# A fourth buffer for the scan units, a third for v, gathers first in a slot

## The chip, the core and the metric

One NeuronCore of a Trainium2 chip runs the whole program. The metric is device time in microseconds (us). Before the change the median of three runs is 211.96 us, with 209.6 and 213.6 as the extremes.

## The reference

A linear-attention recurrence over four sequences (B = 4), eight heads, 768 steps and head size 48, followed by a soft mixture of experts on its output:

```python
for t in range(S):
    cur = einsum('bhd,bhe->bhde', u * k[t], v[t])
    y[t] = einsum('bhd,bhde->bhe', r[t], state + cur)
    state = w[t][..., None] * state + einsum('bhd,bhe->bhde', k[t], v[t])
x = y.transpose(0, 2, 1, 3).reshape(B * S, H * D)        # 3072 x 384
logits = x @ phi                                         # 3072 x 32, 8 experts of 4 slots
d = softmax over tokens;  slot_input = d.T @ x
for e in range(8):
    slot_out[e] = relu(slot_input[e] @ w1[e]) @ w2[e]    # 384 -> 1024 -> 384
out = softmax over slots(logits) @ slot_out
```

Everything is float32.

## The kernel before

The recurrence is cut into chunks of 128 steps, six to a sequence. Decays are turned into running products by scans on VectorE; keys are divided by them and queries multiplied, so that each chunk becomes masked matmuls plus a small state that is carried from chunk to chunk.

**Groups and units.** A sequence has eight heads, worked as four *groups* of two heads (NG = 4); n = 0 to 15 counts the groups of all four sequences. One head takes 48 of 64 partitions, so two heads leave 2 x 16 partitions free. The host packs the fourth group's two heads into these free rows of the first three. So a sequence needs only three *units* of scanning (NU = 3, twelve units in all; `unit(n)` gives a group's unit), and the fourth group's keys and queries are collected afterwards into two tiles of their own, `k3` and `r3`, by `a_gather`: four small DMAs a unit (two from `ld` into `k3`, two from `rt` into `r3`), each from 16 partitions to 16 others.

**Buffers.** `lds` holds a unit's decays and keys (128 x 1550), `rts` its queries (128 x 774); there are three of each, and unit i sits in buffer i % 3. `a_load` fills an `ld`, `a_load_r` an `rt`. `vt` holds a group's values, in a pool of two. VectorE overwrites `ld` and `rt` in place (`a_back` and `a_fwd`, each once for either half h of a unit): the gathers read what `a_fwd(i, 1)` leaves.

**The slots.** The order of all instructions is written out by hand. One pass of the loop over `it` (0 to 16) is called a slot. It scans for the unit of group `it`, does the matmuls of group n = it - 1, and carries the finished output of group m = it - 2 on. In the TensorE order of a slot stand:

- `b_kn` (L292): transposes of the keys, in two halves, which ScalarE copies out (L293, L296);
- `b_scores` (L307): the scores, in two halves of twelve matmuls into two PSUM banks each, that ScalarE copies (L311) and GpSimd masks (L312);
- `d_a` (L246), then `b_u` (L323), whose result VectorE scans into the state (L329) and ScalarE copies (L332);
- `l_turn` (L378): transposes of the finished output x;
- `c_av` (L344), `l_part` (L395), `c_inter` (L359) and two filler matmuls (L782).

`ps_t` is a rotation of four PSUM banks that transposes, scores, `d_a`, `l_turn` and `l_part` share. In the slot of a sequence's fourth group (n = 3, 7, 11, 15) there are no transposes of keys, and the scores read `k3` and `r3`.

**The DMA queue.** All DMAs are issued by SyncE (SP) in program order; a DMA that has to wait holds those behind it. At the head of a slot stand `a_load_v(it)`, `a_load_r` of unit(m) + 3, up to two thirds-of-a-tile of the expert weights (`more_weights`, 512 KB each, PER_IT of them), and then the gathers of unit(n); in the middle of the slot follows `a_load` of unit(n) + 3, into the buffer that was just gathered from. A weight tile is 128 x 3072 (1536 KB). There are sixteen, w1 of eight experts and then w2 of eight; nine arrive in the loop (pool `w_a`, N_WA = 9), two when the decays, keys and queries are finished with and their space is free (`w_b`, N_WB = 2), two when the rest of the recurrence's space is free (`w_c`), three into the first tiles of `w_a` when the first layer has used these.

After the loop come the rest of the logits, the experts' two layers (L530 and L566) and the mixing of their output (L595).

Of the kernel before, what the change touches and what calls it, by code (L numbers as in the profile page):

```python
# [9 lines left out]
F32 = mybir.dt.float32  # L10
# [3 lines left out]
AF = mybir.ActivationFunctionType  # L14
ALU = mybir.AluOpType
# [4 lines left out]
P = 128  # L20
# [7 lines left out]
N_WARM_2 = 5  # L28
N_DENSE = 2
N_FILL = (4, 3)  # L30
N_WA = 9
N_WB = 2
N_WC = 2
N_PIECE = 3
PER_IT = (0, 0, 2, 2, 2, 2, 2, 2, 2, 2, 2, 2, 2, 2, 2, 1)
COLS = ((0, 208), (208, 384))

NB = 4
# [14 lines left out]
def rwkv_soft_moe(ctx: ExitStack, tc: tile.TileContext, wkr, v, ublk, phi, w1, w2, out_a, out_b):  # L53
    nc = tc.nc
    NSC, _, LOAD = wkr.shape
    NIT = v.shape[0]
# [8 lines left out]
    NG = H // 2  # L65
# [4 lines left out]
    SCAN = C * E1  # L70
    R_OFF = K_OFF + SCAN
# [7 lines left out]
    attn = ExitStack()  # L79
    early = ExitStack()  # L80
    decay = early.enter_context(tc.tile_pool(name="decay", bufs=1, side="right"))
    fixed = attn.enter_context(tc.tile_pool(name="fixed", bufs=1))
    once = attn.enter_context(tc.tile_pool(name="once", bufs=1))
    vpool = attn.enter_context(tc.tile_pool(name="vpool", bufs=2))
    work = attn.enter_context(tc.tile_pool(name="work", bufs=4))
    xpool = attn.enter_context(tc.tile_pool(name="xpool", bufs=2))
    ps_y = banks.enter_context(tc.tile_pool(name="ps_y", bufs=1, space=PSUM))
# [2 lines left out]
    ps_c = banks.enter_context(tc.tile_pool(name="ps_c", bufs=1, space=PSUM))  # L90


    lds = [decay.tile([P, R_OFF], F32, name=f"ld{n}") for n in range(3)]
    rts = [decay.tile([P, SCAN], F32, name=f"rt{n}") for n in range(3)]

    def a_load(i, lo=0, hi=R_OFF):
        nc.sync.dma_start(out=lds[i % 3][:, lo:hi], in_=wkr[i, :, lo:hi])

    def a_load_r(i):
        nc.sync.dma_start(out=rts[i % 3], in_=wkr[i, :, R_OFF:LOAD])  # L100
# [9 lines left out]
    b_one = const.tile([P, 1], F32, name="b_one")  # L110
# [56 lines left out]
    prod = cst[:, 4:]  # L167
    up = ps_u.tile([P, D, C], F32, name="up")

    def by_chunk(t):  # L170
        return t.rearrange("p (c e) -> p c e", e=E1)

    def keys(i):
        return by_chunk(lds[i % 3][:, K_OFF:R_OFF])[:, :, 1:E1]

    def queries(i):
        return by_chunk(rts[i % 3])[:, :, 0:P]

    nc.vector.memset(cst[:, 0:1], 1.0)
    nc.vector.memset(cst[:, 1:2], INV_MAX)  # L180
# [11 lines left out]
    def a_load_v(i):  # L192
        vt = vpool.tile([P, 2, C, D], F32, name="vt")
        nc.sync.dma_start(out=vt, in_=v[i])
        sts[i]["vv"] = vt

    def a_back(i, h):

        t, lo = lds[i % 3], HALF * E1 * h
        nc.vector.tensor_tensor_scan(  # L200
            out=prod[:, ::-1], data0=t[:, lo + 1:lo + 1 + HALF * E1][:, ::-1], data1=one,
            initial=1.0, op0=ALU.mult, op1=ALU.min)

        nc.vector.reciprocal(out=by_chunk(t[:, lo:lo + HALF * E1])[:, :, 0], in_=by_chunk(prod)[:, :, 0])

    def a_fwd(i, h):


        lo = HALF * E1 * h
        k_, r_ = lds[i % 3][:, K_OFF + lo:K_OFF + lo + HALF * E1], rts[i % 3][:, lo:lo + HALF * E1]  # L210
        nc.vector.tensor_tensor(out=k_, in0=k_, in1=prod, op=ALU.mult)  # L211
        nc.vector.tensor_tensor_scan(  # L212
            out=prod, data0=lds[i % 3][:, lo:lo + HALF * E1], data1=big, initial=1.0, op0=ALU.mult, op1=ALU.min)
        nc.vector.tensor_tensor(out=r_, in0=r_, in1=prod, op=ALU.mult)  # L214

    def spread(pat, k_):
        pend = by_chunk(k_)[:, 1:C, 0:1].rearrange("p c o -> p o c")
        nc.scalar.copy(out=pat[:, :, 1:C], in_=pend.broadcast_to([P, D, C - 1]))

    def a_pat(i):  # L220
        spread(pats[i % 2], lds[i % 3][:, K_OFF:R_OFF])

    def a_gather(i):

        lo = PART * (i % NU)
        for dst, src in ((k3, lds[i % 3][:, K_OFF:R_OFF]), (r3, rts[i % 3])):
            for h in range(2):
                nc.sync.dma_start(out=dst[64 * h + lo:64 * h + lo + PART], in_=src[64 * h + D:64 * h + 64])

    def a_end(i):  # L230
        junk6 = small.tile([P, C], F32, name="junk6", bufs=1)
        nc.scalar.activation(out=junk6, in_=by_chunk(rts[i % 3])[:, :, P], func=AF.Abs, bias=b_one,
                             scale=1.0, accum_out=chk[:, i:i + 1])

    def d_rk(i):
# [570 lines left out]
    for it in range(NIT + 1):  # L806
        n, m = it - 1, it - 2
        ph = it % NG
        A, i = it < NIT and ph < NU, unit(it)
        B_ = n >= 0  # L810
        mb, mg = divmod(m, NG)
        X = m >= 0 and mg >= 1
        Y = mg == 0 and mb >= 1
        Z = mg == 1 and mb >= 1
        U_ = B_ and n % NG < NU

        nxt = unit(it + 1) if ph == NU and it + 1 < NIT else None
        if 1 <= it < NIT:
            a_load_v(it)
        if m >= 0 and m % NG < NU and unit(m) + 3 < NSC:  # L820
            a_load_r(unit(m) + 3)
        if it < NIT:
            more_weights(it)
        if U_:
            a_gather(unit(n))
        if it == NIT:
            early.close()
            late = weights.enter_context(tc.tile_pool(name="late", bufs=1, side="right", reuse_waits="tile"))
            w_b = weights.enter_context(tc.tile_pool(name="w_b", bufs=N_WB, side="right", reuse_waits="tile"))
            load_weight(w_b, wts, N_WB)  # L830
            cT = late.tile([P, NT // NB, P], F32, name="cT")
            siT = late.tile([P, E * KT, NS], F32, name="siT")
            nc.gpsimd.memset(siT, 0.0)
        if it == 0:
            masks()
            d_rk(0)
            a_back(0, 0)
            a_fwd(0, 0)
            a_back(0, 1)
            d_a(0)  # L840
            d_a_turn(0)
            keep_warm(N_WARM_2, ps_t, "tp")
            d_rk(1)
        if ph == NU:
            d_a_last(it // NG)
        if B_:
            d_av(n)
            b_kn(n, 0)
            b_scores(n, 0)
            b_kn(n, 1)  # L850
        if m >= 0:
            c_evac(m)
        if A and ph == 0:
# [12 lines left out]
        if U_ and unit(n) + 3 < NSC:
            a_load(unit(n) + 3)
        if A and it:
            d_a(i)
        if B_:  # L870
            b_u(n)
        if Y:
            s_exp(mb - 1, qs[mb - 1])
        if B_:
            if not U_:
                spread(pat3, k3)
            b_state(n)
        if X:
            xT = l_turn(xb[mb], mg - 1, once, ps_t)
            if mg == 1:  # L880
                lts[mb] = small.tile([TG, 2, P], F32, name="lt", bufs=1)
        if Z:
            s_norm(mb - 1, qs[mb - 1])
        if A and ph == 0:
            a_back(i + 1, 0)
            a_fwd(i + 1, 0)
        elif A and ph == 1:
            a_back(i + 1, 0)
            d_rk(i + 1)
        elif A:  # L890
            a_fwd(i, 1)
            if it + 2 < NIT:
                d_rk(i + 1)
        elif nxt is not None:
            a_back(nxt, 1)
            d_rk(nxt + 1)
        if it == 1:
            keep_warm(N_WARM_2, ps_t, "tp")
        if B_:
            c_y(n)  # L900
            c_av(n, 0)
            c_av(n, 1)
        if A and it:
            d_a_turn(i)
        if X:
            l_part(mg - 1, xT, lts[mb], ps_t)
        if A:
            a_pat(i)
            a_end(i)
        if X and mg == NG - 1:  # L910
            qs[mb] = s_max(mb, lts[mb], cst[0:TG, 2:3])
        if Y:
            s_dturn(qs[mb - 1], ps_t)
            s_rows(qs[mb - 1], ps_t)
            s_rows_exp(qs[mb - 1])
        if Z and mb < B - 1:
            s_slots(xb[mb - 1], mb - 1, qs[mb - 1], ps_t)
        if B_:
            c_inter(n, 0)
            c_inter(n, 1)  # L920
        if 1 <= it < NIT:
            keep_dense(N_DENSE)
        if Z and mb < B - 1:
            s_sum(mb - 1, qs[mb - 1])
# [184 lines left out]
```

## Time and profile before

| what | value |
|---|---|
| median of 3 runs | 211.96 us (209.6 to 213.6) |
| the profiled execution | 210.83 us, span of its records 209.1 us |
| busy share of the span | PE 87%, PEld 60%, DVE 58%, ACT 44%, POOL 37% |
| share of 16 DMA engines, HBM read | 69.9%, 44.28 MB |
| mean granted TensorE clock | 0.924 |

The profile names engines PE (TensorE matmuls), PEld (its weight loads), DVE (VectorE), ACT (ScalarE), POOL (GpSimd) and SP (SyncE, which only issues DMAs; SPq is its instruction queue). A row of the timeline or of the groups reads: line and engine, operation, output <- inputs, shape, count. The view of waits reads: who waited, for whom, us in total, how often, the longest. The chain of waits follows the work back from the last instruction; its rows read start, length, what. The view by windows gives busy time of each engine in a stretch, with the granted clock (PEclk, 1.00 is full), the DMA engines' busy share and GB/s as its last three columns.

### The profile page before, as it was taken

What the parts mean: (1) busy time and instruction counts of PE and PEld (TensorE: products, weight loads), DVE (VectorE), ACT (ScalarE), POOL (GpSimd) and SP (SyncE); (2) the same over time, 40 slices, a digit from 0 to 9 for tenths busy, and PEclk for the clock granted to TensorE, in tenths of its full rate; (3) what the DMA queues carried; (4) which work ended last, traced back from release to release, by engine and by line L of the source; (5) the groups of instructions that cost most, each with busy time, mean ns of one, the idle gap of its engine ahead of it and who ended that gap; (6) DMA issues with size and microseconds to landing.
All of it is one profiled execution on the core that took longest, in us unless ns stands there. A gap on an engine that the chain in (4) does not pass through costs nothing.

```text
span 209.1 us, 7275 instructions
## 1 busy us (share of the span) xinstructions
PE 181.7 (87%) x3019; PEld 126.0 (60%) x3019; DVE 122.1 (58%) x237; ACT 92.0 (44%) x266; POOL 77.1 (37%) x133
## 2 busy tenths in 40 slices
PE   7599799699999859999982899999969999999830
PEld 2156678477778737777861687788755423565520
DVE  4399859648789861979976088794132531104440
ACT  2043636355777505777750355678524001103330
POOL 3356356532656453274735315464600300000000
PEclk9979759979999996999999579999996999999995
DMA  6975659679595959949587678466888607954873
GB/s 209 358 280 164 187 187 301 231 282 342 163 330 198 324 202 330 325 146 327 188 284 243 225 276 284 96 225 181 304 326 308 263 13 255 419 235 162 330 311 121
DMA packets 14105, 51.93 MB, mean 248 GB/s; under 512 B 2288, under 2 KB 2416, under 8 KB 13552
## 3 DMA queue, kind: packets, MB, share of 16 engines
q1 hardware_dynamic: 14064, 51.38, 69.9%
q8 instruction: 26, 0.43, 0.8%
q14 instruction: 15, 0.12, 0.2%
HBM read 44.28 MB, written 4.72 MB: 234 GB/s over the span
## 4 chain that ended last, share of the span: by engine, by line
PE 67%; DMA 13%; DVE 10%; ACT 2%; issue 2%; SPq 1%; POOL 1%; ACTq 0%; DVEq 0%; POOLq 0%
PE ap L307 14%; DMA r<-rt 10%; PE y L344 8%; PE hp L530 5%; PE so L566 5%; PE tp L378 5%; PE y L359 5%; PE up L323 4%; PE tp L292 3%; PE aps L246 3%; DMA rt<-in_wkr_dram 3%; PE lp L395 3%; PE op L595 2%; DVE cst L200 2%; DVE cst L212 2%
## 5 line engine op out<-in xcount | busy, mean ns | idle before, releaser
L312 POOL TENSOR_SCALAR_AFFINE_SELECT at<-at 128x384 f32<-128x384 f32 x64 | 31.7, 521 | 36.7 <-ACT at L311 36.7
L311 ACT COPY at<-ap 128x384 f32<-128x384 f32 x64 | 27.4, 484 | 25.9 <-PE ap L307 24.9
L307 PE MATMUL ap<-rt,ld 48*128 48x128 f32 x288 | 27.6, 303 | 0.0
L344 PE MATMUL y<-vt,at 128*64 128x48 f32 x768 | 26.6, 228 | 0.0
L344 PEld LDWEIGHTS y<-vt,at 128*64 128x64 f32 x768 | 24.8, 143 | 2.6 <-issue 2.2
L238 POOL TENSOR_TENSOR rk<-rt,ld 128x384 f32<-128x384 f32 x24 | 20.2, 861 | 16.0 <-DMA rt<-in_wkr_dram 14.6
L307 PEld LDWEIGHTS ap<-rt,ld 48*128 48x128 f32 x288 | 22.5, 196 | 4.5 <-issue 4.0
L329 DVE TENSOR_TENSOR_SCAN Sb<-up,pat 112x288 f32<-112x288 f32 x16 | 12.1, 755 | 22.5 <-PE up L323 15.5
L278 POOL TENSOR_TENSOR av<-vt,a 128x576 f32<-128x576 f32 x16 | 18.4, 1151 | 17.0 <-ACT a L257 17.0
L200 DVE TENSOR_TENSOR_SCAN cst<-ld,cst 128x387 f32<-128x387 f32 x24 | 22.9, 954 | 1.6 <-DMA ld<-in_wkr_dram 1.4
L212 DVE TENSOR_TENSOR_SCAN cst<-ld,cst 128x387 f32<-128x387 f32 x24 | 23.2, 968 | 0.8
L332 ACT COPY Sn<-Sb 112x240 f32<-112x240 f32 x16 | 10.1, 632 | 17.4 <-DVE Sb L329 17.4
L307 PE MATMUL ap<-r,k 48*128 48x128 f32 x96 | 9.3, 348 | 9.0 <-DMA r<-rt 9.0
L369 DVE TENSOR_TENSOR x<-y,av 128x576 f32<-128x576 f32 x16 | 12.1, 755 | 6.9 <-PE y L359 5.5
L211 DVE TENSOR_TENSOR ld<-ld,cst 128x387 f32<-128x387 f32 x24 | 13.0, 543 | 3.4 <-POOL rk L238 3.4
L307 PEld LDWEIGHTS ap<-r,k 48*128 48x128 f32 x96 | 8.4, 251 | 9.9 <-issue 9.7
L214 DVE TENSOR_TENSOR rt<-rt,cst 128x387 f32<-128x387 f32 x24 | 13.4, 558 | 0.8
L323 PEld LDWEIGHTS up<-vt,kn 128*48 128x48 f32 x320 | 9.6, 137 | 6.5 <-issue 1.8
L378 PE MATMUL tp<-ident,x 128*128 128x128 f32 x72 | 12.1, 311 | 1.0 <-DVE x L369 1.0
L293 ACT COPY kn<-tp 128x336 f32<-128x336 f32 (+1 forms) x24 | 9.6, 399 | 7.1 <-PE tp L292 7.1
L566 PE MATMUL so<-wt,hT 128*32 128x208 f32 (+1 forms) x256 | 12.5, 329 | 0.0
L380 ACT COPY xT<-tp 128x384 f32<-128x384 f32 x24 | 10.3, 478 | 3.1 <-PE tp L378 3.0
(132 smaller groups left out, 260.2 us busy)
## 6 DMA issues: line engine op xcount, KB each, us to landing
wt<-in_w_dram SPq DMA_DIRECT2D x27, 512.0 KB, 6.8
ld<-in_wkr_dram SPq DMA_DIRECT2D x11, 775.0 KB, 4.3
wt<-in_w_dram SPq DMA_DIRECT2D x4, 1536.0 KB, 7.7
rt<-in_wkr_dram SPq DMA_DIRECT2D x12, 387.0 KB, 6.0
vt<-in_v_dram SPq DMA_DIRECT2D x16, 288.0 KB, 4.5
wt<-in_w_dram SPq DMA_DIRECT2D x3, 832.0 KB, 6.8
out_dram<-wt SPq DMA_DIRECT2D x3, 832.0 KB, 3.8
wt<-in_w_dram SPq DMA_DIRECT2D x3, 704.0 KB, 10.4
```

The source lines that it names most:

```text
L200: nc.vector.tensor_tensor_scan(out=prod[:, ::-1], data0=t[:, lo + 1:lo + 1 + HALF * E1][:, ::-1], data1=one, initial=1.0, op0=ALU.mult, op ...
L212: nc.vector.tensor_tensor_scan(out=prod, data0=lds[i % 3][:, lo:lo + HALF * E1], data1=big, initial=1.0, op0=ALU.mult, op1=ALU.min)
L214: nc.vector.tensor_tensor(out=r_, in0=r_, in1=prod, op=ALU.mult)
L238: nc.gpsimd.tensor_tensor(out=rks[i % 2].rearrange("p (c e) -> p c e", e=P)[:, part], in0=queries(i)[:, part], in1=keys(i)[:, part], op=AL ...
L278: nc.gpsimd.tensor_tensor(out=av, in0=st["vv"], in1=a.broadcast_to([P, 2, C, D]), op=ALU.mult)
L307: nc.tensor.matmul(out=aps[h][:, cc, :], lhsT=kt_[rows, c * E1 + 1:(c + 1) * E1], rhs=rt_[rows, c * E1:c * E1 + P], start=True, stop=True)
L311: nc.scalar.copy(out=at, in_=aps[h])
L312: nc.gpsimd.affine_select(out=at, in_=at, pattern=[[0, 3], [1, P]], compare_op=ALU.is_gt, fill=0.0, base=0, channel_multiplier=-1)
L323: nc.tensor.matmul(out=up[rows, :, n + 1], lhsT=st["kn"][:, n, rows], rhs=st["vv"][:, h, n, :], start=first[h], stop=(n == C - 2))
L344: nc.tensor.matmul(out=st["y"][cols, h, c * D:(c + 1) * D], lhsT=st["AT", h, hf][:, cc, cols], rhs=st["vv"][:, h, c, :], start=(c == 0), s ...
L378: nc.tensor.transpose(out=tp[:, j, :], in_=x[:, 3 * hf + j, kt * P:(kt + 1) * P], identity=ident)
L566: nc.tensor.matmul(out=so[32 * g:32 * g + NS, :], lhsT=hT[ft // 2][:, ft % 2, e, :], rhs=wts[E + e][:, base + ft * wd:base + (ft + 1) * wd ...
```

## The change

`lds` and `rts` get a fourth buffer each (NL = 4), and the pool of `vt` a third. A unit's `ld` and `rt` are now both issued at the head of slot m + 2 for unit(m) + 4, and v for group it + 1 instead of `it`; before the loop v of group 1 and the `ld` and `rt` of unit 3 are loaded as well. The gathers become the first DMAs of a slot, ahead of v, `ld`, `rt` and weights. The space is taken from the loop's weights: N_WA falls from 9 to 8 and N_WB rises from 2 to 3, so that one w2 tile is loaded after the loop instead of in it (PER_IT has three pieces fewer). In `b_kn` and `b_scores` both halves of the key transposes come ahead of the first half of the scores, except in the first group.

```diff
-N_WA = 9
-N_WB = 2
+N_WA = 8
+N_WB = 3
-PER_IT = (0, 0, 2, 2, 2, 2, 2, 2, 2, 2, 2, 2, 2, 2, 2, 1)
+PER_IT = (0, 0, 2, 2, 2, 1, 2, 2, 2, 1, 2, 2, 2, 1, 2, 1)
+NL = 4
-    vpool = attn.enter_context(tc.tile_pool(name="vpool", bufs=2))
+    vpool = attn.enter_context(tc.tile_pool(name="vpool", bufs=3))
-    lds = [decay.tile([P, R_OFF], F32, name=f"ld{n}") for n in range(3)]
-    rts = [decay.tile([P, SCAN], F32, name=f"rt{n}") for n in range(3)]
+    lds = [decay.tile([P, R_OFF], F32, name=f"ld{n}") for n in range(NL)]
+    rts = [decay.tile([P, SCAN], F32, name=f"rt{n}") for n in range(NL)]
...
     a_load_r(2)
     a_load(2)
+    a_load_v(1)
+    a_load(3)
+    a_load_r(3)
     nc.sync.dma_start(out=phi_sb, in_=phi)
...
-        if 1 <= it < NIT:
-            a_load_v(it)
-        if m >= 0 and m % NG < NU and unit(m) + 3 < NSC:
-            a_load_r(unit(m) + 3)
+        if U_:
+            a_gather(unit(n))
+        if 1 <= it < NIT - 1:
+            a_load_v(it + 1)
+        if m >= 0 and m % NG < NU and unit(m) + NL < NSC:
+            a_load(unit(m) + NL)
+            a_load_r(unit(m) + NL)
         if it < NIT:
             more_weights(it)
-        if U_:
-            a_gather(unit(n))
...
             b_kn(n, 0)
+            if n:
+                b_kn(n, 1)
             b_scores(n, 0)
-            b_kn(n, 1)
+            if not n:
+                b_kn(n, 1)
...
             b_scores(n, 1)
-        if U_ and unit(n) + 3 < NSC:
-            a_load(unit(n) + 3)
```

How the order of instructions moves is seen at three places. The first is SP's queue at the head of the slot of n = 6, whose gathers (unit 5, the third of its sequence) are the last that the fourth group n = 7 needs. Numbers at `ld`, `rt` tell the buffers apart; 97 to 99 are the three `ld` of before. Before:

```order
L97 DMA ld_98<-in_wkr_dram 128x1550
L194 DMA vt<-in_v_dram 128x576
L100 DMA rt_101<-in_wkr_dram 128x774
L153 DMA wt<-in_w_dram 128x1024 x2
L228 DMA k_132<-ld_99 16x774 x2
L228 DMA r_133<-rt_102 16x774 x2
```

And the same slot of the changed kernel, where unit 5 sits in `ld_98` and `rt_102`:

```order
L155 DMA wt<-in_w_dram 128x1024 x2
L230 DMA k_134<-ld_98 16x774 x2
L230 DMA r_135<-rt_102 16x774 x2
L196 DMA vt<-in_v_dram 128x576
L99 DMA ld_97<-in_wkr_dram 128x1550
L102 DMA rt_101<-in_wkr_dram 128x774
L155 DMA wt<-in_w_dram 128x1024 x2
```

The four gathers now stand ahead of the slot's v, `ld`, `rt` and two weight pieces, and directly behind the weight pieces of the slot before. The second place is TensorE's order at the head of the slot of n = 8, before:

```order
L292 MATMUL tp<-ident,ld_97 128x128 x3
L307 MATMUL ap<-rt_100,ld_97 128x128 x6
L292 MATMUL tp<-ident,ld_97 128x128 x2
L307 MATMUL ap<-rt_100,ld_97 128x128 x6
L246 MATMUL aps<-rk_129,u_sb 32x256 x3
L323 MATMUL up<-vt,kn 48x48 x10
```

The same slot of the changed kernel (a float32 matmul of these rows is two instructions in the trace):

```order
L294 MATMUL tp<-ident,ld_99 128x128 x5
L309 MATMUL ap<-rt_103,ld_99 128x128 x12
L248 MATMUL aps<-rk_131,u_sb 32x256 x3
L325 MATMUL up<-vt,kn 48x48 x10
L380 MATMUL tp<-ident,x 128x128 x6
```

The five transposes are now one block ahead of one block of twelve scores. The third place is SP's queue around the end of the loop, before:

```order
L153 DMA wt<-in_w_dram 128x1024
L228 DMA k_132<-ld_99 16x774 x2
L228 DMA r_133<-rt_102 16x774 x2
L145 DMA wt<-in_w_dram 128x3072 x4
L145 DMA wt<-in_w_dram 128x1664 x3
L145 DMA wt<-in_w_dram 128x1408 x3
```

And in the changed kernel:

```order
L230 DMA k_134<-ld_100 16x774 x2
L230 DMA r_135<-rt_104 16x774 x2
L155 DMA wt<-in_w_dram 128x1024
L147 DMA wt<-in_w_dram 128x3072 x5
L147 DMA wt<-in_w_dram 128x1664 x3
L147 DMA wt<-in_w_dram 128x1408 x3
```

One more whole weight tile stands between the last gathers and the six part-tiles that end the weights.

More of the change, by code (lines that the diff above doesn't have):

```diff
@@ L90, in rwkv_soft_moe @@
     ps_c = banks.enter_context(tc.tile_pool(name="ps_c", bufs=1, space=PSUM))
-    lds = [decay.tile([P, R_OFF], F32, name=f"ld{n}") for n in range(3)]
-    rts = [decay.tile([P, SCAN], F32, name=f"rt{n}") for n in range(3)]
+    lds = [decay.tile([P, R_OFF], F32, name=f"ld{n}") for n in range(NL)]
+    rts = [decay.tile([P, SCAN], F32, name=f"rt{n}") for n in range(NL)]
     def a_load(i, lo=0, hi=R_OFF):
-        nc.sync.dma_start(out=lds[i % 3][:, lo:hi], in_=wkr[i, :, lo:hi])
+        nc.sync.dma_start(out=lds[i % NL][:, lo:hi], in_=wkr[i, :, lo:hi])
     def a_load_r(i):
-        nc.sync.dma_start(out=rts[i % 3], in_=wkr[i, :, R_OFF:LOAD])
+        nc.sync.dma_start(out=rts[i % NL], in_=wkr[i, :, R_OFF:LOAD])
     a_load(0, 0, K_OFF)
@@ L173, in keys @@
     def keys(i):
-        return by_chunk(lds[i % 3][:, K_OFF:R_OFF])[:, :, 1:E1]
+        return by_chunk(lds[i % NL][:, K_OFF:R_OFF])[:, :, 1:E1]
     def queries(i):
-        return by_chunk(rts[i % 3])[:, :, 0:P]
+        return by_chunk(rts[i % NL])[:, :, 0:P]
     nc.vector.memset(cst[:, 0:1], 1.0)
@@ L197, in a_back @@
     def a_back(i, h):
-        t, lo = lds[i % 3], HALF * E1 * h
+        t, lo = lds[i % NL], HALF * E1 * h
         nc.vector.tensor_tensor_scan(
@@ L209, in a_fwd @@
         lo = HALF * E1 * h
-        k_, r_ = lds[i % 3][:, K_OFF + lo:K_OFF + lo + HALF * E1], rts[i % 3][:, lo:lo + HALF * E1]
+        k_, r_ = lds[i % NL][:, K_OFF + lo:K_OFF + lo + HALF * E1], rts[i % NL][:, lo:lo + HALF * E1]
         nc.vector.tensor_tensor(out=k_, in0=k_, in1=prod, op=ALU.mult)
         nc.vector.tensor_tensor_scan(
-            out=prod, data0=lds[i % 3][:, lo:lo + HALF * E1], data1=big, initial=1.0, op0=ALU.mult, op1=ALU.min)
+            out=prod, data0=lds[i % NL][:, lo:lo + HALF * E1], data1=big, initial=1.0, op0=ALU.mult, op1=ALU.min)
         nc.vector.tensor_tensor(out=r_, in0=r_, in1=prod, op=ALU.mult)
@@ L220, in a_pat @@
     def a_pat(i):
-        spread(pats[i % 2], lds[i % 3][:, K_OFF:R_OFF])
+        spread(pats[i % 2], lds[i % NL][:, K_OFF:R_OFF])
     def a_gather(i):
         lo = PART * (i % NU)
-        for dst, src in ((k3, lds[i % 3][:, K_OFF:R_OFF]), (r3, rts[i % 3])):
+        for dst, src in ((k3, lds[i % NL][:, K_OFF:R_OFF]), (r3, rts[i % NL])):
             for h in range(2):
@@ L231, in a_end @@
         junk6 = small.tile([P, C], F32, name="junk6", bufs=1)
-        nc.scalar.activation(out=junk6, in_=by_chunk(rts[i % 3])[:, :, P], func=AF.Abs, bias=b_one,
+        nc.scalar.activation(out=junk6, in_=by_chunk(rts[i % NL])[:, :, P], func=AF.Abs, bias=b_one,
                              scale=1.0, accum_out=chk[:, i:i + 1])
@@ L271, in rows_of @@
             return k3, r3
-        return lds[unit(i) % 3][:, K_OFF:R_OFF], rts[unit(i) % 3]
+        return lds[unit(i) % NL][:, K_OFF:R_OFF], rts[unit(i) % NL]
     def d_av(i):
```

## The prediction

> **What bounds the kernel now.** I read the page first, for the busy shares and the chain of work that ended last, then that chain in order of time.
>
> ```profile
> PE 181.7 (87%) x3019; PEld 126.0 (60%) x3019; DVE 122.1 (58%) x237; ACT 92.0 (44%) x266; POOL 77.1 (37%) x133
> PE 67%; DMA 13%; DVE 10%; ACT 2%; issue 2%; SPq 1%; POOL 1%; ACTq 0%; DVEq 0%; POOLq 0%
> 34.83 7.16 DMA r<-rt
> ...
> 71.06 6.72 DMA r<-rt
> ...
> 108.20 7.52 DMA r<-rt
> 115.97 3.02 PE ap L307 x24
> ```
>
> TensorE is the bound, and the only DMA of weight in its chain is the gather of `r3`, three times, 6.7 to 7.5 us each: in front of the fourth groups n = 3, 7 and 11. What TensorE really lost is less, since it had other work for most of that time. The view of waits tells it:
>
> ```profile
> PE ap L307 <- DMA r<-rt: 9.0, 3, 4.7
> ```
>
> So 9.0 us of idle TensorE in three waits, 4.7 the longest. Then I looked at the loop by windows: the slots right behind the three waits, then stretches without one (columns: PE, PEld, DVE, ACT, POOL busy, then clock, DMA share, GB/s).
>
> ```profile
> 42.12:50.74 8.62, 8.62 (x156) 6.84 (x157) 4.95 (x9) 4.75 (x13) 3.09 (x5) 0.80 0.87 313
> 77.92:86.70 8.78, 8.78 (x156) 6.86 (x157) 4.21 (x8) 4.97 (x13) 3.14 (x5) 0.81 0.86 305
> 115.97:126.00 10.03, 10.03 (x156) 7.93 (x157) 4.39 (x8) 4.97 (x13) 3.14 (x5) 0.67 0.77 271
> 86.70:101.85 15.15, 15.15 (x312) 12.02 (x311) 13.42 (x24) 10.41 (x32) 8.31 (x13) 1.00 0.80 270
> 126.00:148.28 22.28, 22.27 (x461) 17.74 (x459) 15.60 (x29) 15.59 (x47) 12.32 (x21) 1.00 0.66 193
> ```
>
> Each wait is paid twice: behind it the granted clock averages 0.80, 0.81 and 0.67 over a slot, and elsewhere in the loop it is 1.00 with TensorE busy all the time (15.15 of 15.15, 22.27 of 22.28).
>
> **Why the gather is late.** SP's rows of the slot of n = 6, and the VectorE row that makes the data ready:
>
> ```profile
> 65.15 0.56 DVE L214 TENSOR_TENSOR rt<-rt,cst 128x387 f32<-128x387 f32 x1
> ...
> 67.34 0.33 SPq L97 DMA_DIRECT2D ld<-in_wkr_dram  x1
> 67.80 0.36 SPq L194 DMA_DIRECT2D vt<-in_v_dram  x1
> 68.33 0.33 SPq L100 DMA_DIRECT2D rt<-in_wkr_dram  x1
> 68.71 1.10 SPq L153 DMA_DIRECT2D wt<-in_w_dram  x2
> 69.85 1.16 SPq L228 DMA_DIRECT2D k<-ld  x2
> 71.06 1.30 SPq L228 DMA_DIRECT2D r<-rt  x2
> SPq L97 <- DMA k<-ld: 37.6, 11, 5.9
> DMA to landing us min/median/max: 2.1/5.6/7.5
> ```
>
> Unit 5 is finished at 65.15 + 0.56 = 65.71, but the gather of `r3` is issued at 71.06. SP first sits on the `ld` load, which waits until the gathers have left its buffer (37.6 us over eleven loads), then issues 775 + 288 + 387 + 2 x 512 = 2474 KB in front of the gather, and these have to move first.
>
> **The change part by part.**
>
> *Gathers first, loads a unit ahead.* `r3`'s gathers can go out two k issues (1.16 us) after 65.71, at about 66.9, instead of 71.06. What is ahead of them is the load of the slot before, issued some 8 us earlier. With even the longest landing, 7.5 us, they are there at 74.4; TensorE's own work before them ends at 75.71 (77.92 less the 2.21 it waited). So the wait of n = 7 goes, with 1.3 us to spare in the worst case and 6.7 in the best (2.1 us). Waits on the old buffer go too: the next `ld` now needs a buffer emptied one slot earlier. The same holds at n = 3 and n = 11, which have the same queue. Gain: 9.0 us, all of that wait. What is then late next: nothing on SP, since v, `ld` and `rt` behind the gathers are needed one slot later than before.
>
> *The clock behind the waits.* At full clock the three slots would take 8.62 x 0.80, 8.78 x 0.81 and 10.03 x 0.67, that is 6.9, 7.1 and 6.7 us; the rest, 1.7 + 1.7 + 3.3 = 6.7 us, is the low clock. That the wait causes it is seen at n = 15, a fourth group without a wait:
>
> ```profile
> 148.61 0.92 PE ap L307 x12
> 42.12 1.13 PE L307 MATMUL ap<-r,k 48*128 48x128 f32 x14 [2.06 <-DMA r<-rt]
> 77.92 0.34 PE L307 MATMUL ap<-r,k 48*128 48x128 f32 x1 [2.21 <-DMA r<-rt]
> ```
>
> Its twelve scores take 0.92 us, where the 24 behind the third wait took 3.02 (chain above). I take all 6.7 us; the bounds are 0 and 6.7. [...]
>
> *The order of transposes and scores* (eleven groups: the twelve with transposes less n = 0). The chain at n = 8, and ScalarE's copy there:
>
> ```profile
> 87.03 0.87 PE ap L307 x12
> 87.89 0.37 PE tp L292 x2
> 88.26 1.18 PE ap L307 x12
> 87.98 0.86 ACT L311 COPY at<-ap 128x384 f32<-128x384 f32 x2 [0.34 <-PE ap L307]
> 86.60 0.41 DVE L404 TENSOR_TENSOR lt<-lp,lt 96x256 f32<-96x256 f32 x1
> ```
>
> The second half of the scores takes 0.31 us more than the first. Counting through the four banks of `ps_t`, its second bank is the one that the first half wrote, still being copied at 87.98 to 88.4. In the new order it is a bank of transposes, copied before. At most 11 x 0.31 = 3.4 us. But the first half then reaches back to the bank of `l_part`, which VectorE empties at 86.60 to 87.01, just as that half starts (n = 4, 8, 12), and n = 1, 2 are held by the scans of the start. I count the six groups n = 5, 6, 9, 10, 13, 14: 1.9 us. Against it I put 1.0 us for VectorE being later than now where it has no wait left to catch up in (the `lt` above, three times 0.3). Net gain 0.9, bounds -1.0 and 3.4.
>
> *Loads of the start.* v of group 1 and `ld`, `rt` of unit 3 (1450 KB) stand behind all that the first two units need. What they can delay is phi and the gathers of unit 0, which nothing reads before the slots of n = 2 and 3. I take 0; the bound, if those had no time to spare, is the 4.7 us that 1450 KB take at the 313 GB/s of the first window above.
>
> *The weight tile.* In the loop the DMA engines move three pieces less. After it, 1.57 MB more stand in front of the experts:
>
> ```profile
> 172.76 3.33 SPq L145 DMA_DIRECT2D wt<-in_w_dram  x6
> 146.24:167.00 20.76, 18.67 (x281) 11.91 (x281) 6.63 (x19) 7.30 (x19) 6.12 (x11) 0.92 0.81 302
> 167.00:172.76 5.76, 5.76 (x55) 1.76 (x58) 2.08 (x9) 0.36 (x1) 0.00 (x0) 1.00 0.04 14
> 178.48 0.89 PE L566 MATMUL so<-wt,hT 128*32 128x208 f32 x16
> ```
>
> At 302 GB/s a tile takes 5.2 us. The DMA engines are idle for 5.76 us (share 0.04) before the last six can be issued, and the second layer, the first to use w2, starts at 178.48. So it is hidden by the first layer: 0. With that cover gone it would be 5.2 us.
>
> **The sum.** 9.0 + 6.7 + 1.9 - 1.0 = 16.6 us off the profiled execution's 210.83 (span 209.1 and 1.7 around it): **194.2 us**. That execution lies 0.5% under the median of 211.96, so the sum stands for a middling run. A change under 2% could not be told from none here.
>
> **Rivals.**
>
> *VectorE becomes the bound.* Two groups of four slots, and the stretches with the lowest and the highest share of VectorE:
>
> ```profile
> 42.12:77.92 35.80, 32.80 (x627) 25.34 (x628) 27.41 (x49) 20.16 (x59) 18.30 (x29) 0.95 0.77 269
> 77.92:115.97 38.05, 32.67 (x628) 25.18 (x628) 27.59 (x50) 20.57 (x60) 18.38 (x29) 0.95 0.74 253
> 33.00:42.12 9.12, 6.85 (x148) 5.35 (x147) 7.03 (x12) 4.34 (x12) 4.89 (x8) 1.00 0.77 273
> 58.90:65.89 6.99, 6.99 (x153) 5.74 (x152) 6.62 (x11) 4.89 (x15) 4.41 (x9) 1.00 0.97 360
> ```
>
> Without wait and low clock the two groups would take 35.80 - 2.2 - 1.7 = 31.9 and 38.05 - 4.7 - 1.7 = 31.6 us, with 27.41 and 27.59 us of VectorE in them, 86 to 87%. It does 6.62 of 6.99 us (95%) in a slot where TensorE never waits for it: for the forecast. In 33.00 to 42.12 it did 77%. If it can hold only that, a group takes 27.5 / 0.77 = 35.7 us, 3.8 and 4.1 us are lost again: 202.1 us.
>
> *The low clock stays behind the first two places.* Were its cause there not the short wait but something in the fourth group itself, 1.7 + 1.7 us would stay: 197.6 us. Against it stands n = 15. [...]
>
> *The change does not do what it says:* the gathers still land too late, because the loads of the slot before fill the engines. It would need a landing of 8.8 us (75.71 - 66.9); none of 24 took over 7.5. Time as now, about 210.
>
> *Slower: the granted clock falls under steady load.* Without waits TensorE would run unbroken from 33 to about 132 us, where the trace shows 22.28 us at most. At a clock c this stretch of 99 us grows by 99 x (1/c - 1), which eats 16.6 us at c = 0.856; at the 0.80 seen above it is 24.8: 219 us. Against it: no drop in the trace without a wait ahead of it.
>
> **Chances.** Forecast 0.62, VectorE 0.17, clock stays 0.08, gathers still late 0.07, slower 0.06. The range goes from 190.5 (9.0 + 6.7 + 3.4 off is 191.7, less 0.6% for the run) to 202.5, which takes in the first two rivals: 0.87. Faster by over 2% 0.87, the same 0.07, slower 0.06.
>
> **What would show it.** The wait of the scores for `r<-rt` gone from the view of waits (9.0 to under 1); a clock near 1.00 in the loop from 33 us on; the fourth groups' slots near 7 us; the second half of the scores as short as the first; no wait of L566 for weights. I am wrong if VectorE's share in the loop passes 90% and TensorE waits for it (L329's state, x or `lt`), if the gather's landing grows past its slot, or if the clock drops without a wait.

## The result, and the profile after

| | before | after |
|---|---|---|
| median of 4 runs each on one chip | 211.90 us (209.60 to 213.60) | 190.78 us (190.40 to 191.53) |
| ratio, 95% interval | | 0.904 (0.896 to 0.912) |
| the profiled execution, its span | 210.83, 209.1 us | 191.53, 189.8 us |
| mean granted TensorE clock | 0.924 | 0.972 |

The change makes the kernel about 9.6% faster here, and 7.6% faster on a second chip (below). The forecast was 194.2 us, with a range of 190.5 to 202.5. Medians below are over all runs of a kernel, while ratios leave out the runs that took over 1.5% longer than that kernel's fastest, so the two need not agree to the last per cent.

First the page: busy times and the summary of the chain of work that ended last.

```profile
PE 167.4 (88%) x3019; PEld 117.3 (62%) x3019; DVE 121.2 (64%) x237; ACT 90.0 (47%) x266; POOL 76.7 (40%) x133
PE 42%; DVE 24%; DMA 11%; ACT 8%; issue 7%; POOL 2%; SPq 1%; ACTq 0%; DVEq 0%; POOLq 0%
```

TensorE does the same 3019 matmuls in 14.3 us less busy time (181.7 before): most of that is clock, as the windows below show, and none of it is work left out. Its share of the chain falls from 67% to 42% and VectorE's rises from 10% to 24%. The chain changes hands, but the engine with the highest busy share is still TensorE.

The view of waits, first three rows of TensorE after, and below them the row of before that answers to the first:

```profile
PE lp L397 <- ACT xT L382: 3.6, 10, 0.9
PE aps L248 <- POOL rk L240: 2.1, 1, 2.1
PE ap L309 <- ACT kn L298: 1.4, 1, 1.4
```
```profile
PE lp L395 <- ACT xT L380: 2.5, 4, 0.9
```

The row `ap <- DMA r<-rt` (9.0, 3, 4.7 before) is gone. The longest sum is now the logits' wait for ScalarE's copy of x: 2.5 us in four waits before, 3.6 in ten after. Why the gather is in time, in SP's and TensorE's timelines around the slot of n = 6 and the head of n = 7, and in the view of the tile `r`:

```profile
57.01 1.15 SPq L230 DMA_DIRECT2D k<-ld  x2
58.61 2.13 SPq L230 DMA_DIRECT2D r<-rt  x2
60.85 0.52 SPq L196 DMA_DIRECT2D vt<-in_v_dram  x1
68.57 1.61 PE L309 MATMUL ap<-r,k 48*128 48x128 f32 x24
DMA to landing us min/median/max: 2.1/3.1/5.4
```

The gather is issued by 60.74 and lands at most 5.4 us later; the scores start at 68.57 with no idle time in front of them (it would stand in brackets). The median landing falls from 5.6 to 3.1 us, with the same four small DMAs. By windows (columns as in the prediction), the three fourth-group slots, then the two groups of four slots for which the prediction gave 31.9 and 31.6 us:

```profile
36.39:43.68 7.29, 7.04 (x159) 5.35 (x155) 6.17 (x10) 4.67 (x13) 3.10 (x5) 1.00 1.03 409
68.25:75.57 7.32, 7.04 (x159) 5.36 (x155) 6.18 (x10) 4.71 (x13) 3.10 (x5) 1.00 0.98 379
99.86:107.17 7.31, 7.04 (x160) 5.35 (x155) 6.32 (x12) 4.68 (x13) 3.10 (x5) 1.00 0.62 224
43.68:75.57 31.89, 30.46 (x634) 23.86 (x628) 26.87 (x49) 19.78 (x59) 18.21 (x29) 1.00 0.87 305
75.57:107.17 31.60, 30.00 (x632) 23.66 (x628) 27.13 (x50) 19.77 (x60) 18.19 (x29) 1.00 0.75 254
```

The clock is 1.00 in all five, and VectorE works 26.87 of 31.89 us (84%) and 27.13 of 31.60 (86%) without slowing the groups.

**Where the 19.3 us went.** The two filler matmuls that end every slot mark the slots in both traces; the differences of their starts, summed by kind of slot, for the two profiled executions:

| stretch | before | after | difference | forecast |
|---|---|---|---|---|
| start to the end of n = 0 | 22.70 | 22.04 | -0.66 | 0 |
| n = 1 | 9.40 | 6.35 | -3.05 | none |
| n = 3, 7, 11 (fourth groups) | 36.40 | 21.92 | -14.48 | -15.7 |
| n = 4, 5, 8, 9, 12, 13 | 45.45 | 43.65 | -1.80 | -1.9 (for other slots) |
| n = 2, 6, 10, 14 | 34.27 | 35.38 | +1.11 | +1.0 (VectorE) |
| n = 15 to the first expert matmul | 18.72 | 17.18 | -1.54 | none |
| experts to the end | 42.16 | 43.28 | +1.12 | 0 |
| sum | 209.1 | 189.8 | -19.30 | -16.6 |

So 2.7 us more came off than forecast. The rows without a forecast, n = 1 and n = 15 onward, give 4.6 us; nearly all of it is low clock that the profile of before has and that of after hasn't:

```profile
22.70:32.10 9.40, 9.40 (x153) 7.41 (x148) 6.63 (x10) 4.39 (x15) 4.63 (x10) 0.64 0.60 185
156.00:161.00 5.00, 4.74 (x26) 2.83 (x26) 0.91 (x4) 1.67 (x4) 0.00 (x0) 0.66 0.84 315
```
```profile
15.00:20.00 5.00, 5.00 (x61) 2.69 (x60) 4.79 (x9) 1.65 (x6) 3.40 (x6) 0.66 0.81 238
```

Before (upper fence), 9.40 x 0.36 = 3.4 us are lost to the clock in slot n = 1, and 5.00 x 0.34 = 1.7 in the tail. After (lower fence), only one such piece is left where TensorE works, 5.00 x 0.34 = 1.7 us, inside the slot of n = 0. It is half clock, since windows of one microsecond inside such pieces read 0.50; this one is from before:

```profile
26.00:27.00 1.00, 1.00 (x13) 0.78 (x11) 0.91 (x2) 0.10 (x1) 0.42 (x1) 0.50 0.99 401
```

The 3.4 us do not show in full: where the clock is full in slot n = 1, the old order takes 6.66 us there (the experiment with fillers in the waits) and the new one 6.35. So 2.74 of the 3.05 us are clock and 0.31 are the order. The experiments show that the 2.74, and the 1.54 of the tail, are not the change's own. Without them 15.0 us come off, which is 1.6 less than the forecast and not 2.7 more.

### The profile page after: what moved, and what is told of

It reads as the page before. It is cut to its first block, busy times and chain, and to the rows that moved or that the text cites. A ratio compares the mean times of both kernels' runs of the same rounds, so it can differ in the third digit from the quotient of the medians.

```text
span 189.8 us, 7288 instructions
## 1 busy us (share of the span) xinstructions
PE 167.4 (88%) x3019; PEld 117.3 (62%) x3019; DVE 121.2 (64%) x237; ACT 90.0 (47%) x266; POOL 76.7 (40%) x133
## 4 chain that ended last, share of the span: by engine, by line
PE 42%; DVE 24%; DMA 11%; ACT 8%; issue 7%; POOL 2%; SPq 1%; ACTq 0%; DVEq 0%; POOLq 0%
PE ap L309 7%; DVE cst L214 7%; PE hp L532 6%; PE so L568 6%; DVE cst L202 4%; DMA ld<-in_wkr_dram 4%; DVE ld L213 3%; DVE Sb L331 3%; PE y L346 3%; DMA wt<-in_w_dram 3%; PE y L361 3%; PE op L597 3%; DMA rt<-in_wkr_dram 3%; ACT at L313 2%; PE lp L397 2%
## 5 line engine op out<-in xcount | busy, mean ns | idle before, releaser
L313 ACT COPY at<-ap 128x384 f32<-128x384 f32 x64 | 26.8, 492 | 11.7 <-PE ap L309 10.8
L309 PE MATMUL ap<-rt,ld 48*128 48x128 f32 x288 | 23.9, 288 | 3.1 <-ACT kn L298 1.4
L346 PE MATMUL y<-vt,at 128*64 128x48 f32 x768 | 25.5, 223 | 0.0
L346 PEld LDWEIGHTS y<-vt,at 128*64 128x64 f32 x768 | 23.7, 138 | 2.3 <-issue 1.6
L309 PEld LDWEIGHTS ap<-rt,ld 48*128 48x128 f32 x288 | 20.7, 187 | 5.6 <-issue 1.8
L216 DVE TENSOR_TENSOR rt<-rt,cst 128x387 f32<-128x387 f32 x24 | 13.4, 558 | 0.8
L325 PEld LDWEIGHTS up<-vt,kn 128*48 128x48 f32 x320 | 8.8, 128 | 6.2 <-issue 5.3
L380 PE MATMUL tp<-ident,x 128*128 128x128 f32 x72 | 10.5, 282 | 0.9 <-DVE x L371 0.9
L532 PE MATMUL hp<-wt,siT 128*32 128x512 f32 x96 | 11.0, 596 | 0.0
L361 PEld LDWEIGHTS y<-Sn,rt 48*64 48x64 f32 x480 | 8.3, 134 | 4.3 <-issue 3.6
```

The lines of the kernel that those rows point to most:

```text
L309: nc.tensor.matmul(out=aps[h][:, cc, :], lhsT=kt_[rows, c * E1 + 1:(c + 1) * E1], rhs=rt_[rows, c * E1:c * E1 + P], start=True, stop=True)
L313: nc.scalar.copy(out=at, in_=aps[h])
L346: nc.tensor.matmul(out=st["y"][cols, h, c * D:(c + 1) * D], lhsT=st["AT", h, hf][:, cc, cols], rhs=st["vv"][:, h, c, :], start=(c == 0), s ...
L532: nc.tensor.matmul(out=hp[32 * g:32 * g + NS, :], lhsT=siT[:, e * KT + kt, :], rhs=wts[e][:, kt * F + hf * 512:kt * F + hf * 512 + 512], s ...
```

## The experiments

Two accounts were to be told apart first. The prediction's is that the place of the gathers in SP's queue causes waits and low clock; the rival is that the fourth buffer and the loads a unit ahead bring the gain. A second question is what the order of transposes and scores is worth, a third what sets off the half clock in the places that the prediction had not counted.

**The gathers' place alone, in the kernel before.**

```diff
+        if U_:
+            a_gather(unit(n))
         if 1 <= it < NIT:
             a_load_v(it)
...
             more_weights(it)
-        if U_:
-            a_gather(unit(n))
```

> The kernel before with nothing changed but the gathers' place: first in a slot, ahead of v, rt and weights. Theory A (the wait comes from the 2474 KB that are issued ahead of the gather): the wait of the scores for r is under 1.5 us in all instead of 9.0, the low clock behind it goes with it, and the time is 193 to 198. Theory B (the three buffers make SP wait for the old gathers, 37.6 us, and only the fourth frees it): the gather still lands late, the wait is 5 us or more, and the time is 204 or more.

Measured: 192.28 us (190.60 to 195.65), ratio 0.915 (0.904 to 0.927). The slots n = 3, 7 and 11 take 7.29, 7.30 and 7.31 us, as in the changed kernel, and the first row of TensorE's waits, with the landing of `r`, is

```profile
PE lp L395 <- ACT xT L380: 2.8, 6, 0.9
DMA to landing us min/median/max: 2.1/3.0/7.4
```

None of the three waits for `r` is left. The time lies just under the 193 to 198 expected. With three buffers, two for v and nine tiles in the loop, these lines moved carry nearly the whole gain.

**Everything but the gathers' place**: the changed kernel with the gathers put back behind v, `ld`, `rt` and the weights.

```diff
-        if U_:
-            a_gather(unit(n))
         if 1 <= it < NIT - 1:
             a_load_v(it + 1)
...
             more_weights(it)
+        if U_:
+            a_gather(unit(n))
```

> The changed kernel with the gathers put back behind v, ld, rt and the weights of their slot; the buffers, the loads a unit ahead, the weight tile and the order of transposes stay. Theory A: the gathers are again behind 2474 KB, about 6 to 7 us of transfer, so the scores wait 1 to 3 us in front of each fourth group, the clock falls behind most of them, and the time is 197 to 206. Theory B: no wait, the time of the changed kernel, 191.

Measured: 212.34 us (211.23 to 215.17), ratio 1.014 (1.003 to 1.026). Waits, landing, SP's rows in front of the second wait, and TensorE's row there:

```profile
PE ap L309 <- DMA r<-rt: 13.4, 3, 5.5
DMA to landing us min/median/max: 2.1/5.6/7.9
70.56 0.33 SPq L99 DMA_DIRECT2D ld<-in_wkr_dram  x1
71.07 0.33 SPq L102 DMA_DIRECT2D rt<-in_wkr_dram  x1
71.45 1.20 SPq L155 DMA_DIRECT2D wt<-in_w_dram  x2
72.69 1.18 SPq L230 DMA_DIRECT2D k<-ld  x2
73.92 1.96 SPq L230 DMA_DIRECT2D r<-rt  x2
80.80 3.19 PE L309 MATMUL ap<-r,k 48*128 48x128 f32 x24 [3.64 <-DMA r<-rt]
```

The gathers again stand behind 775 + 387 + 2 x 512 KB, the landing is back at 5.6 us, and the waits grow to 13.4. That the kernel is no faster at all was not expected (197 to 206): buffers without the gathers' new place are worth nothing or less. The two kernels together show from both sides that the gathers' place decides. They do not part the two reasons that the prediction gave for it. In this kernel, too, SP stands still before it issues the `ld` loads, until the gathers of the slot before have landed (20.8 us in five waits, 4.0 of them just ahead of the 70.56 above), and ahead of its loads of v it waits 40.4 us in all, ten times, for TensorE to be done with a buffer. How much of the lateness is this standing still and how much is the transfer of the bulk loads is not shown.

**The old order of transposes and scores in the changed kernel.**

```diff
             b_kn(n, 0)
-            if n:
-                b_kn(n, 1)
             b_scores(n, 0)
-            if not n:
-                b_kn(n, 1)
+            b_kn(n, 1)
```

> The changed kernel with the transposes and scores in the old order (three transposes, six scores, two transposes, six scores). If the order was worth what the slots of the two traces show (six groups faster by 0.2 to 0.4 us, four slower by 0.2 to 0.4), this run is 0.5 to 1.5 us slower than the changed kernel, about 192. If the order is where the unforecast 4 us came from, it is 3 to 5 us slower, about 195. If the slower groups (n = 2, 6, 10, 14) are slow because of VectorE and not because of the order, they stay slow here.

Measured: 196.17 us (195.17 to 196.61), ratio 0.939 (0.931 to 0.947). In the slots n = 1 to 14 the old order takes 1.95 us more than the changed kernel. A further 3.75 us lie between n = 15 and the experts, where nothing of this edit stands: the window there, and TensorE's row just ahead of the drop.

```profile
139.00:146.00 7.00, 6.16 (x28) 3.75 (x28) 1.48 (x5) 2.29 (x6) 0.00 (x0) 0.52 0.89 315
139.84 1.54 PE L380 MATMUL tp<-ident,x 128*128 128x128 f32 x6 [0.94 <-DVE x L371]
```

7.00 x 0.48 = 3.4 us of half clock, right behind an idle time of 0.94 us that the changed kernel has too, at full clock (`tp <- x`, 0.9 to 1.0 us in either). So the comparison of this run with the changed kernel's is mostly one of where half clock fell, and the order itself is worth some 2 us. The median lies above either expectation (192 and 195), as neither counted both parts.

**Fillers in that stretch**, six ahead of the last `l_part` of the loop and eight behind the last `c_inter`, in the old order and in the changed kernel (the same lines in both):

```diff
+        if it == NIT:
+            keep_dense(6)
         if X:
             l_part(mg - 1, xT, lts[mb], ps_t)
...
-        if 1 <= it < NIT:
-            keep_dense(N_DENSE)
+        if 1 <= it:
+            keep_dense(N_DENSE if it < NIT else 8)
```

> The changed kernel with the old order of transposes and scores (196.2 us) plus filler matmuls in the two short idle times at the end of the loop (6 before the logits of the last slot, 8 after its last output matmuls). Theory: of the 5.4 us that the old order costs, about 3.7 us are a half clock from 139 to 146 us, set off by these idle times of 0.7 to 0.9 us; with them filled the clock stays 1.00 and the time is 192 to 193. Rival: the half clock has to do with the order itself; then the time stays at 195 to 197.

> The changed kernel with the same fillers at the end of its loop, where its clock was 1.00 without them. Theory: nothing to win in its usual runs, so 190.5 to 191.5; only if some of its runs fall into the half clock is it faster. If filling delays the last logits it is up to 1 us slower.

Measured: 194.35 us (193.78 to 196.59), ratio 0.925 (0.918 to 0.932) in the old order; 192.24 us (191.16 to 195.49), ratio 0.916 (0.909 to 0.922) in the changed kernel. In the old order the half clock of the tail is gone and the median 1.8 us lower, though on another chip, and short of the 192 to 193 expected. The profiled executions with and without these fillers have nearly the same span, 194.8 and 194.9 us: with them, half clock lies in n = 0 instead (15.00 to 23.00 us, 8.00 x 0.43 = 3.4 us), and n = 0 ends at 24.19 us, not at 21.41. In the changed kernel, whose tail had none, the stretch takes 18.4 instead of 17.18 us: the fillers cost 1.2 us and are worth nothing. The two kernels with fillers, which differ by the order alone, lie 2.1 us apart.

**Fillers in the waits**, in the kernel before: 20 more filler matmuls at the end of the slots n = 2, 6 and 10, ahead of the waits for `r`.

```diff
         if 1 <= it < NIT:
-            keep_dense(N_DENSE)
+            keep_dense(N_DENSE + (20 if ph == NU and it < NIT - 1 else 0))
```

> The kernel before with 20 more filler matmuls at the end of the slots of n = 2, 6 and 10, where TensorE waits 2.06, 2.21 and 4.68 us for the gather. The waits for the gather stay, but TensorE is busy in the first two and for half of the third. If the wait causes the low clock behind it, the clock behind the first two is 1.00 and each is 1.7 us shorter, the third keeps some or all of its 3.3: time 205 to 209 against 211.9. If the clock falls for another reason in the fourth groups, it is still about 0.8 there and the time is 211 or more, by what the fillers overrun.

Measured: 209.79 us (207.82 to 213.69), ratio 0.998 (0.989 to 1.007). The three waits in TensorE's timeline, and a window around each:

```profile
39.96 1.73 PE L307 MATMUL ap<-r,k 48*128 48x128 f32 x24 [0.79 <-DMA r<-rt]
77.83 2.12 PE L307 MATMUL ap<-r,k 48*128 48x128 f32 x24 [2.87 <-DMA r<-rt]
115.57 2.25 PE L307 MATMUL ap<-r,k 48*128 48x128 f32 x24 [2.34 <-DMA r<-rt]
39.00:45.00 6.00, 5.20 (x99) 4.18 (x97) 2.18 (x4) 3.23 (x8) 1.94 (x4) 1.00 0.72 251
78.00:84.00 6.00, 6.00 (x92) 4.71 (x93) 1.92 (x4) 3.77 (x9) 1.94 (x4) 0.72 0.88 323
115.00:121.00 6.00, 5.43 (x68) 4.17 (x70) 1.09 (x2) 2.90 (x7) 1.99 (x4) 0.72 0.77 271
```

Behind 0.79 us of idle time the clock stays at 1.00. Behind 2.87 us, and behind 2.34, it averages 0.72 over six, 6.00 x 0.28 = 1.7 us lost; the third loss is half of before's 3.3, as the wait is half of its 4.68. So the low clock goes with the waits: it followed the 2.06 us of before at n = 3, and did not follow the 0.79 us that are left of them here. The fillers did not shorten the second wait, against the expectation. They take back the time that they give, and the total stays.

This run also answers for slot n = 1. Its edit begins at the end of n = 2, so up to there it is the kernel of before, but its slot n = 1, from one row of fillers to the next, takes 6.66 us at a clock of 1.00 where the profile of before has 9.40:

```profile
21.07 0.39 PE L782 MATMUL up<-zb 128*128 128x256 bf16 x2
27.73 0.39 PE L782 MATMUL up<-zb 128*128 128x256 bf16 x2
```

**The start shifted**: the changed kernel with the queries of unit 3 loaded first of all, which nothing needs so early.

```diff
+    a_load_r(3)
     a_load(0, 0, K_OFF)
...
     a_load(3)
-    a_load_r(3)
```

> The changed kernel with the queries of unit 3 loaded first of all instead of last ahead of the loop, which delays the first scan and so the whole loop by 1.0 to 1.3 us against the start of the program. If where the half clock falls depends only on the idle times, the time is the changed kernel's plus this, 191.8 to 192.2. [...]

Measured: 193.47 us (192.18 to 194.70), ratio 0.919 (0.911 to 0.928). By windows:

```profile
23.00:31.00 8.00, 8.00 (x118) 6.61 (x109) 5.74 (x9) 3.89 (x12) 4.44 (x8) 0.57 0.86 321
10.00:14.00 4.00, 3.54 (x16) 1.53 (x16) 3.83 (x7) 1.16 (x3) 2.80 (x3) 0.57 1.02 415
```

n = 0 ends 1.07 us later (23.11), and slot n = 1 takes 9.06 us instead of 6.35, with 8.00 x 0.43 = 3.4 us of half clock: the picture of before in a kernel that has all of the change. So the half clock of n = 1 is no matter of buffers, gathers or order: it came in a kernel that has all three, and was missing in the run above, which has none. That the shift sets it off is not shown. Two of the four executions took 194.7 and 194.5 us, the other two 192.4 and 192.2, about what the shift alone would give, and the profiled one is the slowest.

**Gathers and order without buffers**, on two chips, the second time beside the changed kernel itself. The edit is the one of the first experiment and the new order in `b_kn` and `b_scores`.

> The kernel before with two edits: gathers first in a slot, and the new order of transposes and scores. No fourth buffer, no third v, no load a unit ahead, no weight tile moved. If the buffers and the loads ahead bring nothing once the gathers are first, this takes 190 to 192 us like the changed kernel (the order is worth about 2 us in the slots). If the buffers carry part of the gain that is hidden in the scatter of the first round, it is 193 us or more.

> The gathers first and the new order alone, a second time, on one chip with the changed kernel. Theory, that buffers, loads ahead and tile are worth nothing: the same median as the changed kernel to within 1 us, 189.5 to 191.5. Rival, that the earlier loads keep the slots from waiting: 1.5 to 3 us slower than the changed kernel, with a slot of 9 us or more at n=3, 7 or 11.

> The changed kernel once more, as the measure of the three others on the same chip: 190.4 to 191.5 as before, with 7.3 us in slots n=3, 7 and 11.

Measured: 192.57 us (189.54 to 196.63), ratio 0.905 (0.898 to 0.912), the first time. On the second chip 190.38 us (189.04 to 192.35), ratio 0.910 (0.901 to 0.918), against 193.79 us (190.60 to 194.71), ratio 0.924 (0.916 to 0.932), for the changed kernel and 212.24 for before. Without the buffers it is as fast, by the medians 3 us faster, though the intervals of the ratios overlap. The first time, its profile is that of its slowest execution: TensorE stands idle for 2.82 us inside the scores of n = 2, and the profile names nothing that it waited for; 3.4 us of half clock follow (32.00 to 42.00 us, 10.00 x 0.34). The second profile has neither. The changed kernel's own repeat missed its expectation of 190.4 to 191.5: its ratio on this chip lies above the first one's interval. The change's gain is thus 7.6 to 9.6%, and differs by more between the two occasions than either interval allows. In the profiled executions (spans 187.3 and 188.9) the slots n = 1 to 14 take 106.59 and 106.80 us; 0.34 us of the difference lie in the start and 1.04 behind the experts' first matmul. There the rows are alike up to the last copy of the output on ScalarE:

```profile
179.35 0.31 ACT L601 COPY wt<-op 128x176 f32<-128x176 f32 x1
```
```profile
179.90 0.31 ACT L603 COPY wt<-op 128x176 f32<-128x176 f32 x1
```

Without the buffers (upper) the span ends 7.6 us after that copy, with them (lower) 8.7: the last stores and the end of the program. Six of the eight profiles with the buffers have 8.6 to 8.9 us there, and all six without them 7.3 to 7.9. The two exceptions (the gathers put back, the start shifted) have 7.7, and in both TensorE stands idle for 1.0 us inside the scores of n = 15 instead. So the buffers may cost 1 us there; no run here tests why.

**Fillers at the start**: five more warming matmuls and five fillers behind the scores of n = 0, in the changed kernel and in the one without buffers.

```diff
-N_WARM = 16
+N_WARM = 21
...
             if not n:
                 b_kn(n, 1)
+                keep_dense(5)
```

> The changed kernel with five more warming matmuls ahead of the first slot (21 instead of 16) and five filler matmuls behind the score halves of slot n=0, so that TensorE has work in its idle times of 2.06 us and 1.38 us at the start. Theory one, that these idle times set off the half clock of 15 to 19 us: the half clock at the start goes, the profiled execution loses 1.7 us and the median is 188.5 to 189.5. [...]

> The kernel before with the gathers first and the new order of transposes and scores, without the buffers, the loads ahead and the tile, and with the same two fillers at the start. If buffers and loads ahead bring nothing, it gives the same as the changed kernel with these fillers to within 1 us (188.5 to 192). If a fourth buffer is worth something once the start is dense, it is 1 to 3 us slower than that one.

Measured: 195.12 us (192.17 to 196.10), ratio 0.921 (0.908 to 0.934) with the buffers; 193.37 us (192.03 to 195.56), ratio 0.919 (0.911 to 0.928) without. By the medians both are slower than the same kernel without the fillers, by 1.3 and 3.0 us, though the intervals of the ratios overlap; neither median lies in the range expected. Two windows of the kernel without buffers, with fillers and (lower fence) without; under the windows TensorE's row at the end of n = 0:

```profile
14.00:20.00 6.00, 5.40 (x93) 3.71 (x93) 5.79 (x10) 2.19 (x7) 3.63 (x6) 1.00 0.71 205
20.00:32.00 12.00, 11.15 (x187) 9.43 (x187) 7.81 (x13) 5.64 (x17) 5.12 (x9) 0.57 0.74 232
20.84 1.32 PE L359 MATMUL y<-Sn,rt 48*64 48x48 f32 x40 [1.44 <-ACT Sn L332]
```
```profile
14.00:20.00 6.00, 6.00 (x85) 3.66 (x85) 5.79 (x10) 2.02 (x8) 3.64 (x6) 0.72 0.74 210
20.00:32.00 12.00, 11.87 (x258) 9.99 (x254) 11.09 (x18) 8.77 (x27) 7.95 (x14) 1.00 0.77 252
20.63 0.80 PE L359 MATMUL y<-Sn,rt 48*64 48x48 f32 x40
```

With the fillers the clock is 1.00 from 14 to 20 us, but TensorE then has 1.44 us to wait for the state, and the half clock comes afterwards: 12.00 x 0.43 = 5.2 us. Without fillers the half clock falls into n = 0 (6.00 x 0.28 = 1.7 us) and takes the place of that wait, so that it costs nothing: the row begins 0.21 us earlier. The same wait stands in the profile of before, where half clock follows it in n = 1, and in that of the old order, where none does (lower fence):

```profile
21.97 0.80 PE L359 MATMUL y<-Sn,rt 48*64 48x48 f32 x40 [1.44 <-ACT Sn L332]
```
```profile
20.68 0.80 PE L361 MATMUL y<-Sn,rt 48*64 48x48 f32 x40 [1.44 <-ACT Sn L334]
```

The theory that filling the idle times at the start takes the half clock away fell. With the buffers, too, it came later: in the profile of the changed kernel with these fillers it lies at the end of n = 0 (20.00 to 25.00 us, 5.00 x 0.34 = 1.7 us) and in the tail (139.00 to 145.00 us, 6.00 x 0.28 = 1.7). The half clock of the tail thus comes in a kernel that has the whole change.

## Why the prediction was right, and where it was off

- **Gathers first (9.0 us).** Right, and shown both ways: moved alone they take the waits away; everything else without the move leaves 13.4 us. The prediction credited the loads a unit ahead with part of it, a free buffer one slot earlier; the runs give that nothing.
- **The clock behind the waits (6.7 us).** Right in full: the first three windows of after stand at 1.00. Half clock followed waits of 2.06 and 2.21 us in the kernel before, and of 2.34 and 2.87 with the fillers in the waits, 1.7 us lost behind each; behind the 4.68 of before it was 3.3.
- **The fourth-group slots** were put at 6.9, 7.1 and 6.7 us and take 7.29, 7.32 and 7.31, which makes 1.2 us of the 15.7. Their row of the logits shows 0.8 of it, a wait that came in the place of the old one, 0.25, 0.28 and 0.27 us at n = 3, 7 and 11; the second of them:

```profile
74.27 0.63 PE L397 MATMUL lp<-xT,phi_sb 128*32 128x256 f32 x6 [0.28 <-ACT xT L382]
```

- **Order (1.9 us).** The sum fits (1.80 in the slots, 1.95 when undone), the slots don't. The prediction excluded n = 4, 8, 12, because their first half would reach back to the bank of `l_part`, and counted n = 6, 10 and 14. The gain came at n = 4, 5, 8, 9, 12, 13, of 0.20 us in the first of each pair and 0.39 in the second, and at n = 1 (0.31). In TensorE's timeline, the first transpose and the `d_a` behind the scores of n = 8, before (upper) and after:

```profile
86.53 0.49 PE L292 MATMUL tp<-ident,ld 128*128 128x128 f32 x3
89.37 0.63 PE L246 MATMUL aps<-rk,u_sb 128*32 128x256 f32 x6
```
```profile
75.80 0.71 PE L294 MATMUL tp<-ident,ld 128*128 128x128 f32 x5
78.18 0.63 PE L248 MATMUL aps<-rk,u_sb 128*32 128x256 f32 x6
```

  2.84 us become 2.38, and no idle time stands ahead of the scores, so nothing is seen of the feared bank of `l_part`. Part of the 0.46 is given back in the wait for xT of that slot (0.17 us).
- **VectorE lateness (1.0 us).** The size is about right, +1.11 us in n = 2, 6, 10 and 14, but its cause isn't shown: the wait that grew (2.5 to 3.6 us) names ScalarE's copy, behind x of VectorE. With the old order n = 10 and 14 are back at 9.42 and 7.46 us while n = 2 and 6 stay slow at 8.33 and 10.02, so it has at least two parts, and the order itself is one of them.
- **Loads of the start and the weight tile (0 and 0).** Right as far as seen; the 1.12 us that came on behind the first expert matmul come from the stretch after the last copy (above), and their cause is open. The second layer waits for no weights, though the DMA engines' idle stretch is shorter than the 5.76 us of before:

```profile
148.00:152.00 4.00, 4.00 (x41) 1.14 (x34) 1.71 (x6) 0.36 (x1) 0.00 (x0) 1.00 0.02 4
158.06 0.89 PE L568 MATMUL so<-wt,hT 128*32 128x208 f32 x16
```

- **The step that failed** is the sentence that elsewhere in the loop the clock is 1.00: it was read from 33 us on. Slot n = 1 and the tail lie outside, and their half clock, 2.74 and 1.54 us of the difference, was counted neither as a gain nor as a scatter. This is what puts the 190.78 at the low end of the range, and that it stays inside is luck: that end allowed 3.4 us for the order, not for the clock. Neither piece is the change's to keep: the kernel of before can lack the first (fillers in the waits), and the changed kernel can have either (shifted start, fillers at the start). Other runs of the changed kernel took up to 194.7 us, so that the forecast of 194.2 lies within what this kernel does.
- **The rivals.** VectorE as the bound would have given 35.7 us to a group; they took 31.89 and 31.60. The low clock did not stay behind the first two places, the gathers were not late, and TensorE ran at 1.00 through both groups, from 43.68 to 107.17 us, so steady load did not lower the clock there.

## What to carry to other kernels

Where a small transfer on the critical path shares a queue with bulk loads, move it ahead of them before spending space on buffers: here moving one call gave what the new buffers alone did not (192.28 against 212.34 us). Price a wait of TensorE with the low clock behind it, which here cost 0.6 to 0.8 of the wait once more (1.7 us behind waits of 2.06, 2.21, 2.34 and 2.87, 3.3 behind 4.68), and nothing behind 0.79. And before a few per cent are credited to an edit, mark equal stretches in both traces and set apart those that differ only by clock.

## What the runs showed of the hardware

- At half clock (0.50 in windows of one microsecond), each place found where TensorE works lost 1.7 us or 3.4 (5.00 x 0.34 in the tail of before, 9.40 x 0.36 in its n = 1, 7.00 x 0.48 in the old order), and 5.2 in one case (fillers at the start, without buffers). What sets these sizes was not shown.
- The length of an idle time alone did not decide. An idle time of 0.94 us in the old order was followed by a drop of 3.4 us, while the changed kernel went through a like one (0.95 us) at a clock of 1.00. The 1.44 us at the end of n = 0 were followed by a drop in some profiles (3.4 us in that of before, 5.2 with fillers at the start and without buffers) and by none in that of the old order. Even 2.06 us, ahead of TensorE's row at 8.84 us in the changed kernel, were followed by a clock of 1.00 from 10 to 15 us, where the 2.06 us of before at n = 3 brought a drop of 1.7. What else decides was not shown.
- A drop cost nothing where it fell on a stretch that had a wait without it: in n = 0 of the kernel without buffers, 1.7 us of half clock took the place of a wait of 1.44 us, and the row behind it began 0.21 us earlier. In the profile with fillers there, half clock of 5.2 us came later instead.
